# A retention layer fused with a two-layer MLP: two chunks' products with v per visit, the running state in fp32 on VectorE, a block-diagonal v for the short chunk

## The chip, the cores and the metric

The kernel runs on one NeuronCore of one Trainium2 chip. The core has a matrix engine (TensorE, PE; its weight loads are shown as PEld), VectorE (DVE), ScalarE (ACT), GpSimd (POOL) and SyncE (SP, which only issues transfers here). They run side by side, each in its own program order, and wait for one another by semaphores. The metric is device time in microseconds, smaller is better. All times below are in microseconds unless ns is written.

## What is computed

Per batch (8) and head (8), with 576 positions of 64 numbers, q, k and v give a causal product with decay. Its result, 4608 tokens of 512 numbers, goes through two matrix products with a nonlinear step between them:

```python
gamma = 1.0 - 2.0 ** (-5.0 - np.arange(H))
Dmat = np.where(rel >= 0, gamma[:, None, None] ** rel[None], 0.0)   # rel = i - j
attn = np.matmul(scale * np.matmul(q, k.T) * Dmat, v)
x = attn.transpose(0, 2, 1, 3).reshape(B * S, H * D)                 # 4608 x 512
h = x @ w_in                                                         # 512 x 2048
out = (h * np.cos(h)) @ w_out                                        # 2048 x 512
```

## The kernel before

**Chunks.** The positions of a batch are cut into chunks r = 0 to 4: four of 128 and a last one of 64, the short chunk. The decay is put into v (WV) and q (UP, UPN) ahead of time, so that a chunk needs four products, each for four pairs of heads c and the two heads hp of a pair:
- `scores` (line 515): k times q within the chunk, 64 contraction rows per head, into two PSUM banks (one per hp); `mask` (line 536), two VectorE multiplies with a triangular mask, writes them to RT as bf16
- `sums_q` (line 562): q times the state of all chunks before, a 128 by 128 block-diagonal state per pair (SB, bf16)
- `sums_v` (line 573): the masked scores times v, into the same PSUM bank as `sums_q`, and the copy of the sum to XT (the MLP's input)
- `state` (line 598): k times v, accumulated over the chunks in the PSUM bank ST; two ScalarE copies bring it to SB as bf16

`rest` (line 549) does sums_q, sums_v, state and the copies for one chunk. XT is copied by VectorE there (line 595), the state by ScalarE (line 616).

**The MLP.** Tokens go in nine blocks j of 512. `mlp1` (line 629) makes one of 16 column tiles of the hidden layer: four matmuls of 512 columns, the cosine on ScalarE (line 644), the product with h on VectorE (line 647). `mlp2` (line 654) makes a quarter of an output tile st (four of 16 matmuls of 512 columns); four quarters make one of four output tiles, which ScalarE copies out (osb, line 681), and `flush` stores from ScalarE's queue.

**PSUM.** Eight banks of 128 by 512 fp32: SC0 and SC1 (scores), PO (sums), ST (state), and four MM banks that `bank()` (line 212) hands out in turn, leaving out the one that an unfinished output tile holds. Nothing plans this: the order of the program is the order of each engine, and a bank is reused as soon as its last reader has signalled.

**The order around the change** is written out by hand in `emit` (line 714). In the loop over j from 1 on, the attention of batch b = j + 1 stands between the 16 quarters n of mlp2:
- j = 1 (batch 2): the short chunk of batch 1 and the scores of chunk 0 at n = 2, then one chunk and the next chunk's scores at n = 5, 8, 11, 14 (`stage`, line 622). For n under 8 two narrow mlp1 tiles of 192 columns (line 856) go ahead of each quarter
- j = 2 to 6 (batches 3 to 7): the short chunk of batch b - 1 and the scores of chunks 0 and 1 at n = 0; one chunk each at n = 4, 7, 10, 13; the scores of 2 and 3 behind n = 7's, of chunk 4 behind n = 13's. The second score pair of n = 0 and n = 7 takes two MM banks (line 850)
- j = 7: the short chunk of batch 7

**Inputs.** SP's queue loads k, q and v per chunk as fp32 (`load`, line 284). POOL casts k and multiplies q and v (`prep`, line 373), and SP's transposing transfers write KQT. `feed` does this one batch ahead, behind mlp1's tiles. Batches 0 and 1 have paths of their own through PE transposes.

Of the kernel before, what the change touches and what calls it, by code (L numbers as in the profile page):

```python
# [48 lines left out]
class Sched:  # L49


    def __init__(self, nc, es):
        self.nc, self.es = nc, es
        self.eng = {
            "dve": nc.vector, "act": nc.scalar, "pool": nc.gpsimd,
            "pe": nc.tensor, "sp": nc.sync,
        }
        self.sem = {k: es.enter_context(nc.semaphore(f"p_{k}")) for k in ("dve", "act", "pool", "pe")}
        self.count = dict.fromkeys(self.sem, 0)
        self.seen = {k: {} for k in self.eng}  # L60
# [38 lines left out]

    def op(self, eng, fn, reads=(), writes=()):  # L100
        self.waits(eng, reads, writes)
        return self.done(eng, fn(self.eng[eng]), reads, writes)
# [22 lines left out]
class _Kernel:  # L125
    def __init__(self, nc, es, q, k, v, w_in, w_out, out):
# [7 lines left out]
        def sb(name, shape, dt):  # L134
# [26 lines left out]
        self.VB = [[sb(f"vb{i}_{r}", [128, DM], BF16) for r in range(NCH)] for i in range(2)]  # L161
        self.bVB = [[Buf() for _ in range(NCH)] for _ in range(2)]
        self.RT = [[sb(f"rt{i}_{hp}", [128, 512], BF16) for hp in range(2)] for i in range(2)]
        self.bRT = [[Buf() for _ in range(2)] for _ in range(2)]
        self.SB = [sb(f"sb{i}", [128, NP * 128], BF16) for i in range(3)]
        self.bSB = [Buf() for _ in range(3)]
        self.GT = [sb(f"gt{i}", [128, 16 * TB], BF16) for i in range(2)]

# [10 lines left out]
        self.IG = sb("ig", [128, S_], F32)  # L179
        self.IP = sb("ip", [128, NCH], F32)  # L180
        self.UP = sb("up", [128, NP * S_], F32)
        self.WV = sb("wv", [128, NCH * H_], F32)
        self.UPN = sb("upn", [128, NCH * H_], F32)
        self.LW = sb("lw", [128, NCH * H_], F32)
        self.MK = sb("mk", [128, CH], BF16)
        self.ID = sb("ident", [128, 128], BF16)
        self.ZERO, self.bZERO = sb("zero", [128, 512], BF16), Buf()
# [41 lines left out]
    def consts_a(self):  # L229

        s = self.s
        bj = Buf()
        s.op("dve", lambda e: e.memset(self.JUNK.ap(), 0.0), writes=[bj])
        s.op("act", lambda e: e.activation(self.JUNK2.ap(), self.JUNK.ap(), AF.Exp), reads=[bj])
        s.op("pool", lambda e: e.iota(self.IP.ap(), [[CH, NCH]], base=0, channel_multiplier=1,
                                      allow_small_or_imprecise_dtypes=True), writes=[self.bIP])
# [12 lines left out]
        s.op("dve", lambda e: e.memset(self.C_PIH.ap(), float(math.pi / 2.0)), writes=[self.bC])  # L249
        for h in range(H_):  # L250
            s.op("dve", lambda e: e.tensor_scalar_mul(
                bass.AP(self.LW, h, [[NCH * H_, 128], [H_, NCH]]), self.IP.ap(), self.lng[h]),
                reads=[self.bIP], writes=[Buf()])
        self.bLW.w = [Tok("dve", "dve", s.count["dve"], {})]
        for i in range(3):
            s.op("dve", lambda e: e.memset(self.SB[i].ap(), 0.0), writes=[self.bSB[i]])

    def consts_n(self):
# [98 lines left out]
    def mul(self, eng, x, r, t, o, pitch, w, bw, bt):  # L357
# [3 lines left out]
            self.staged(x, r, [[D_, H_], [1, D_]]),  # L361
            bass.AP(w, r * H_, [[NCH * H_, ck], [1, H_], [0, D_]]), ALU.mult),
            reads=[self.bST32[x][r], bw], writes=[bt])
# [151 lines left out]
    def scores(self, b, r, later=False, sc=None):  # L515

        s, ck, i, q0 = self.s, ck_of(r), b % 2, CH * r
        sc = sc or list(zip(self.SC, self.bSC))
        mms = []
        for c in range(NP):  # L520
# [7 lines left out]
        self.group(mms, [self.bKT[i][r], self.bQT[i][r]], [sc[0][1], sc[1][1]])  # L528
        k = self.rt[b, r] = len(self.rt) % 2
        for hp in range(2):  # L530
# [12 lines left out]
    def masked(self, b, r, c, hp, ck):  # L543

        if b == 0 and r < NCH - 1:
            return bass.AP(self.GT[1], (2 * c + hp) * TB + r * CH, [[16 * TB, ck], [1, ck]])
        return bass.AP(self.RT[self.rt[b, r]][hp], c * CH, [[512, ck], [1, ck]])
# [8 lines left out]
    def sums(self, b, r, po=None, eng="dve"):  # L556

        if r:
            self.sums_q(b, r, po)
        return self.sums_v(b, r, po, eng)  # L560

    def sums_q(self, b, r, po=None):

# [5 lines left out]
                     bass.AP(self.KQT[i], TQ + c * S_ + q0, [[TP, 128], [1, ck]]),  # L569
                     dict(start=c == 0, stop=False, skip_group_check=True)) for c in range(NP)],  # L570
                   [self.bSB[(r - 1) % 3], self.bQT[i][r]], [bpo])

    def sums_v(self, b, r, po=None, eng="dve"):

        s, ck, i, q0 = self.s, ck_of(r), b % 2, CH * r
        po, bpo = po or (self.PO, self.bPO)
        mms = []
        for c in range(NP):
            for hp in range(2):
# [4 lines left out]
                    self.masked(b, r, c, hp, ck),  # L584
                    dict(start=r == 0 and c == 0, stop=c == NP - 1, skip_group_check=True)))
        reads = [self.bVB[i][r]]
        if b == 0 and r < NCH - 1:
# [4 lines left out]
        t0 = (b * S_ + q0) % XR  # L592
# [3 lines left out]
        return lambda: s.op(eng, fn, reads=[bpo], writes=self.bXT[t0 // GR:(t0 + ck) // GR])  # L596

# [23 lines left out]

    def stage(self, b, r):
        self.rest(b, r)
        if r + 1 < NCH:
            self.scores(b, r + 1)

# [87 lines left out]
    def emit(self):  # L714
# [138 lines left out]

# [38 lines left out]
```

## Time and profile before

| | |
|---|---|
| median of 3 runs | 312.69 (312.68 to 313.04) |
| the profiled execution | 312.78 |
| its span, first to last instruction | 311.0 |
| TensorE clock granted, mean | 0.995 of full |
| DMA engines, mean busy share | 9 tenths or more for slices 2 to 26 of 40 |
| VectorE: rt from sc, 128x512 | 36 of 682 ns |
| VectorE: xt from po, 128x512 | 26 of 691 ns |
| ScalarE: sb from st, 64x256 | 64 of 377 ns |
| ScalarE: osb from mm, 128x512 | 35 of 597 ns |

A page of the profile has the busy time of each engine, the span in 40 slices, the chain of work that ended last (followed back from the last instruction to what released each step), and the costliest groups of instructions by line. Besides it the trace answers with timelines (start, length, engine, line, operation, output from inputs, shapes, and in brackets the idle time before with what ended it). On VectorE neighbouring instructions overlap a little, so a start-to-start distance is shorter than a length.

### The profile page before, as it was taken

To read this page: it belongs to the slowest core of one execution; us is meant where nothing else is said; L and a number is where in the kernel's file an instruction comes from. 1 tells how busy PE (TensorE), PEld (TensorE's weight loads), DVE (VectorE), ACT (ScalarE), POOL (GpSimd) and SP (SyncE) were. 2 spreads that over 40 slices of the span, in tenths; PEclk is the share of its full clock that TensorE was granted. 3 is DMA by queue.
4 is the path that set the end of the run, shared out by engine and by line. 5 is a ranking of instruction groups with operands and counts; after the bars stand their busy time and mean duration, and the time that the engine had idled before them with its cause. 6 is when DMAs were issued, how large, how long until landed. Compare 5 with 4: busy or idle time off the path is not lost.

```text
span 311.0 us, 6450 instructions
## 1 busy us (share of the span) xinstructions
PE 303.1 (97%) x2538; PEld 159.0 (51%) x2538; DVE 178.3 (57%) x318; ACT 161.2 (52%) x288; POOL 106.5 (34%) x129
## 2 busy tenths in 40 slices
PE   6799999999999999999999999999999999999996
PEld 3574455666644455445544554455445554444444
DVE  5857644887548842785368554855487448405800
ACT  8658407875447433753277236723573347316711
POOL 4881046645565636354646554510000000000000
PEclk9979999999999999999999999999999999999999
DMA  7999999999999999999999998950101010120022
GB/s 230 252 198 208 208 216 247 250 229 182 249 222 179 233 208 228 181 229 200 251 195 221 237 222 195 191 136 34 36 0 70 34 36 0 40 98 0 1 76 95
DMA packets 138319, 49.12 MB, mean 158 GB/s; under 512 B 127921, under 2 KB 132273, under 8 KB 138289
## 3 DMA queue, kind: packets, MB, share of 16 engines
q1 hardware_dynamic: 128880, 34.88, 61.8%
q10 hardware_dynamic: 5184, 9.31, 8.9%
q0 software_dynamic: 4224, 4.52, 8.7%
q8 instruction: 20, 0.33, 0.5%
q14 instruction: 11, 0.08, 0.1%
HBM read 36.70 MB, written 9.44 MB: 148 GB/s over the span
## 4 chain that ended last, share of the span: by engine, by line
PE 92%; SPq 3%; DMA 2%; ACT 1%; DVE 0%; issue 0%; ACTq 0%
PE mm L511 62%; PE mm L513 20%; PE po L511 5%; PE sc L511 3%; DMA qn<-in_moe_w_in_dram 2%; SPq L288 2%; SPq L296 1%; PE st L511 1%; ACT osb L681 1%; PE po L513 0%; ACT kqt L415 0%; DVE win L330 0%; DVE xt L595 0%; ACT xt L595 0%; ACT sb L616 0%
## 5 line engine op out<-in xcount | busy, mean ns | idle before, releaser
L647 DVE TENSOR_TENSOR gt<-mm,cb 128x512 bf16<-128x512 f32 (+3 forms) x164 | 101.6, 626 | 61.2 <-ACT cb L644 58.6
L511 PE MATMUL mm<-xt,win 128*128 128x512 bf16 (+3 forms) x492 | 119.1, 353 | 0.5 <-DVE xt L595 0.4
L644 ACT ACTIVATE cb<-mm,c_pih 128x512 bf16<-128x512 f32 (+3 forms) x164 | 102.8, 636 | 31.1 <-PE mm L513 30.7
L511 PE MATMUL mm<-wout,gt 128*128 128x512 bf16 (+1 forms) x450 | 117.4, 373 | 0.0
L511 PEld LDWEIGHTS mm<-xt,win 128*128 128x128 bf16 x492 | 46.4, 98 | 48.8 <-DVE xt L595 1.0
L511 PEld LDWEIGHTS mm<-wout,gt 128*128 128x128 bf16 x450 | 41.0, 98 | 42.2 <-DVE gt L647 0.2
L513 PE MATMUL mm<-xt,win 128*128 128x512 bf16 (+3 forms) x164 | 57.9, 353 | 0.0
L513 PE MATMUL mm<-wout,gt 128*128 128x512 bf16 (+1 forms) x142 | 53.6, 378 | 0.0
L681 ACT ACTIVATE osb<-mm 128x512 f32<-128x512 f32 x35 | 20.9, 597 | 62.5 <-PE mm L513 62.5
L359 POOL TENSOR_TENSOR vb<-vn,wv 128x512 bf16<-128x512 f32 (+1 forms) x40 | 41.6, 1042 | 11.3 <-DMA vn<-in_v_dram 10.1
L595 DVE CAST xt<-po 128x512 bf16<-128x512 f32 (+1 forms) x34 | 21.3, 627 | 40.5 <-PE po L513 40.5
L370 POOL CAST kqb<-kn 128x512 bf16<-128x512 f32 (+1 forms) x35 | 21.3, 610 | 66.7 <-DMA kn<-in_k_dram 61.7
L616 ACT ACTIVATE sb<-st 64x256 bf16<-64x256 f32 x64 | 24.2, 377 | 35.7 <-PE st L513 34.7
L359 POOL TENSOR_TENSOR kqb<-qn,upn 128x512 bf16<-128x512 f32 (+1 forms) x30 | 31.3, 1042 | 14.5 <-DMA qn<-in_q_dram 13.6
L538 DVE TENSOR_TENSOR rt<-sc,mk 128x512 bf16<-128x512 f32 (+1 forms) x52 | 29.1, 597 | 6.5 <-PE sc L513 6.5
L513 PEld LDWEIGHTS mm<-xt,win 128*128 128x128 bf16 x164 | 16.0, 98 | 15.4
L513 PEld LDWEIGHTS mm<-wout,gt 128*128 128x128 bf16 x142 | 13.9, 98 | 16.5
L511 PE MATMUL po<-rt,vb 128*64 128x128 bf16 (+1 forms) x245 | 13.6, 220 | 0.0
L538 DVE TENSOR_TENSOR rt<-mm,mk 128x512 bf16<-128x512 f32 x20 | 12.8, 681 | 0.0
L511 PEld LDWEIGHTS po<-rt,vb 128*64 128x64 bf16 (+1 forms) x245 | 8.3, 108 | 5.5 <-DVE rt L538 2.1
L511 PE MATMUL sc<-kqt 64*128 64x128 bf16 (+1 forms) x196 | 10.3, 213 | 0.8 <-ACT kqt L415 0.8
L511 PE MATMUL st<-vb,kqb 128*64 128x64 bf16 x224 | 9.5, 198 | 1.5 <-POOL vb L359 0.8
(126 smaller groups left out, 166.5 us busy)
## 6 DMA issues: line engine op xcount, KB each, us to landing
out_dram<-osb ACTq DMA_DIRECT2D x35, 256.0 KB, 3.4
vn<-in_v_dram SPq DMA_DIRECT2D x32, 256.0 KB, 5.1
kn<-in_k_dram SPq DMA_DIRECT2D x28, 256.0 KB, 4.1
qn<-in_q_dram SPq DMA_DIRECT2D x24, 256.0 KB, 4.6
wout<-in_moe_w_out_dram POOLq DMA_DIRECT2D x4, 512.0 KB, 15.7
kn<-in_k_dram SPq DMA_DIRECT2D x4, 288.0 KB, 5.1
qn<-in_q_dram SPq DMA_DIRECT2D x4, 288.0 KB, 5.4
vn<-in_v_dram SPq DMA_DIRECT2D x8, 128.0 KB, 4.3
```

The source lines that it names most:

```text
L288: return self.s.dma(eng, f"{x}n{r}", lambda e: e.dma_start(dst, src), writes=[self.bST32[x][r]], after=after)
L296: self.s.dma("sp", f"{x}0_{c}", lambda e: e.dma_start(dst, src), writes=[self.bN0[x][c]])
L359: self.s.op(eng, lambda e: e.tensor_tensor(bass.AP(t, o, [[pitch, ck], [D_, H_], [1, D_]]), self.staged(x, r, [[D_, H_], [1, D_]]), bass.A ...
L370: fn = (lambda e: e.activation(o, f, AF.Copy)) if eng == "act" else (lambda e: e.tensor_copy(o, f))
L511: self.nc.tensor.matmul(o, a, b, **kw)
L513: return s.done("pe", self.nc.tensor.matmul(o, a, b, **kw), reads, writes)
L538: self.s.op("dve", lambda e: e.tensor_tensor(bass.AP(self.RT[k][hp], 0, p3), bass.AP(sc[0], 0, p3), bass.AP(self.MK, 0, [[CH, ck], [0, NP] ...
L595: fn = (lambda e: e.activation(o, f, AF.Copy)) if eng == "act" else (lambda e: e.tensor_copy(o, f))
L616: s.op("act", lambda e: e.activation(bass.AP(self.SB[r % 3], 64 * hp * 512 + 64 * hp, [[512, 64], [128, NP], [1, D_]]), bass.AP(self.ST, 6 ...
L644: s.op("act", lambda e: e.activation(co, mo, AF.Sin, bias=self.C_PIH.ap(), scale=1.0), reads=[bm, self.bC], writes=[bcb])
L647: s.op("dve", lambda e: e.tensor_tensor(bass.AP(g, dt * TB + o, [[16 * TB, 128], [1, n]]), mo, co, ALU.mult), reads=[bm, bcb], writes=bg[o ...
L681: s.op("act", lambda e: e.activation(o.ap(), m.ap(), AF.Copy), reads=[bm], writes=[bo])
```

## The change

1. **Two chunks per visit.** For batches 2 to 7, chunks 0 and 1 go together, and 2 and 3. `two` issues the q-times-state of the first, k times v of both (`kv`), the products with v of both, the scores that come next, and leaves the second chunk's q-times-state and its XT copy to `then`, which is called one or two quarters later. The second chunk's sums go to an MM bank.
2. **State in fp32.** k times v of each chunk is no longer accumulated in PSUM: each chunk has a half of ST, VectorE adds it to a running sum in SBUF (S32), and ScalarE copies that to SB (`add`).
3. **XT copies** of these chunks go to ScalarE.
4. **The short chunk.** Its scores of both heads of a pair are stacked in one bank (rows 0 to 63 and 64 to 127), masked by one VectorE instruction with a mask of its own (MK4), and multiplied with a block-diagonal v: four 128*128 matmuls (`sums_4`) in place of eight of 64*64. Its v is loaded by two transfers into the two halves of the rows, and multiplied by two POOL instructions of half the width; a POOL instruction that follows the second half, and the second half itself, wait for POOL's instruction before.
5. **Constants**: an extra column in IP, LW, WV, UPN for the second half, two zeroed v tiles, MK4.

The diff, cut to its core:

```diff
-    def op(self, eng, fn, reads=(), writes=()):
+    def op(self, eng, fn, reads=(), writes=(), shifted=False):
+        if eng == "pool":
+            if shifted or self.shifted:
+                self.need(eng, Tok(eng, eng, self.count[eng], {}))
+            self.shifted = shifted
...
+        for i in range(2):
+            s.op("dve", lambda e: e.memset(self.VB[i][NCH - 1].ap(), 0.0), writes=self.bV4[i])
+        for hp in range(2):
+            s.op("dve", lambda e: e.tensor_copy(
+                bass.AP(self.MK4, 64 * hp * 64, [[64, 64], [1, 64]]),
+                bass.AP(self.MK, 64 * hp * CH + 64 * hp, [[CH, 64], [1, 64]])),
...
     def scores(self, b, r, later=False, sc=None):
+        if r == NCH - 1:
+            m, bm = sc[0]
+            mms = []
+            for c in range(NP):
+                for hp in range(2):
+                    base = 64 * hp * TP + c * S_ + q0
+                    mms.append((
+                        bass.AP(m, 64 * hp * 512 + c * ck, [[512, ck], [1, ck]]),
...
+    def sums_4(self, b, r, po=None, eng="dve"):
+        ck, i, k = ck_of(r), b % 2, self.rt[b, r]
+        po, bpo = po or (self.PO, self.bPO)
+        self.group([(bass.AP(po, c * CH, [[512, 128], [1, ck]]),
+                     bass.AP(self.VB[i][r], c * 128, [[DM, 128], [1, 128]]),
+                     bass.AP(self.RT[k][0], c * ck, [[512, 128], [1, ck]]),
+                     dict(start=False, stop=c == NP - 1, skip_group_check=True))
+                    for c in range(NP)], self.bV4[i] + [self.bRT[k][0]], [bpo])
+        return self.evict_x(b, r, po, bpo, eng)
...
+    def kv(self, b, r):
+        i, o = b % 2, 256 * (r % 2)
...
+                    dict(start=not o and c == 0, stop=c == NP - 1, skip_group_check=True)))
+        self.group(mms, [self.bKB[i][r], self.bVB[i][r]], [self.bST])
+
+    def add(self, r):
+        s, k = self.s, r % 2
+        o = self.S32[k].ap()
+        f = self.ST[:, 256 * k:256 * k + 256]
+        if r == 0:
+            s.op("dve", lambda e: e.tensor_copy(o, f), reads=[self.bST], writes=[self.bS32[k]])
+        else:
+            s.op("dve", lambda e: e.tensor_tensor(o, f, self.S32[1 - k].ap(), ALU.add),
+                 reads=[self.bST, self.bS32[1 - k]], writes=[self.bS32[k]])
+        for hp in range(2):
+            s.op("act", lambda e: e.activation(
+                bass.AP(self.SB[r % 3], 64 * hp * 512 + 64 * hp, [[512, 64], [128, NP], [1, D_]]),
+                bass.AP(self.S32[k], 64 * hp * 256, [[256, 64], [D_, NP], [1, D_]]), AF.Copy),
+                reads=[self.bS32[k]], writes=[self.bSB[r % 3]] if hp else [Buf()])
+
+    def two(self, b, r, nxt):
+        if r:
+            self.sums_q(b, r)
+        self.kv(b, r)
+        self.kv(b, r + 1)
+        po = self.bank()
+        done = self.sums_v(b, r, eng="act")
+        self.sums_v(b, r + 1, po, first=True)
+        self.add(r)
+        done()
+        for k, sc in nxt:
+            self.scores(b, k, sc=sc and sc())
+        self.add(r + 1)
+
+        def then():
+            self.sums_q(b, r + 1, po, first=False)
+            self.evict_x(b, r + 1, *po, "act")()
+        return then
+
+    def both(self):
+        return [self.bank(), self.bank()]
...
+            at = (8, 13) if j == 1 else (5, 11)
...
-                if j == 1:
-                    if n == 2:
-                        self.rest(1, NCH - 1)
-                        self.scores(2, 0)
-                    elif n % 3 == 2:
-                        self.stage(2, n // 3 - 1)
-                elif n == 0 and b <= B_:
+                if n == (1 if j == 1 else 0) and b <= B_:
                     self.rest(b - 1, NCH - 1)
-                if 1 < j < B_ - 1:
-                    if n in (4, 7, 10, 13):
-                        self.rest(b, n // 3 - 1)
-                    if n in (0, 7):
-                        self.scores(b, n // 3)
-                        self.scores(b, n // 3 + 1, sc=[self.bank(), self.bank()])
-                    elif n == 13:
-                        self.scores(b, NCH - 1)
+                if j < B_ - 1:
+                    if j == 1 and n == 3:
+                        self.scores(b, 0)
+                        self.scores(b, 1, sc=[(self.PO, self.bPO), (self.ST, self.bST)])
+                    elif j > 1 and n == 0:
+                        self.scores(b, 0)
+                        self.scores(b, 1, sc=self.both())
+                    if n == at[0]:
+                        then = self.two(b, 0, [(2, None), (3, self.both)])
+                    elif n == at[1]:
+                        then = self.two(b, 2, [(4, None)])
+                    elif n in (at[0] + 1, at[1] + 2):
+                        then()
```

More of the change, by code (lines that the diff above doesn't have):

```diff
@@ L17 @@
 NCH = (S_ + CH - 1) // CH
+NW = NCH + 1
 TOK = B_ * S_
@@ L61, in __init__ @@
         self.dsem = {}
+        self.shifted = False
     def need(self, eng, tok):
@@ L162, in __init__ @@
         self.bVB = [[Buf() for _ in range(NCH)] for _ in range(2)]
+        self.bV4 = [[Buf(), Buf()] for _ in range(2)]
+        self.bS4 = [Buf(), Buf()]
         self.RT = [[sb(f"rt{i}_{hp}", [128, 512], BF16) for hp in range(2)] for i in range(2)]
@@ L166, in __init__ @@
         self.bSB = [Buf() for _ in range(3)]
+        self.S32 = [sb(f"s32_{i}", [128, NP * D_], F32) for i in range(2)]
+        self.bS32 = [Buf(), Buf()]
         self.GT = [sb(f"gt{i}", [128, 16 * TB], BF16) for i in range(2)]
@@ L179, in __init__ @@
         self.IG = sb("ig", [128, S_], F32)
-        self.IP = sb("ip", [128, NCH], F32)
+        self.IP = sb("ip", [128, NW], F32)
         self.UP = sb("up", [128, NP * S_], F32)
-        self.WV = sb("wv", [128, NCH * H_], F32)
-        self.UPN = sb("upn", [128, NCH * H_], F32)
-        self.LW = sb("lw", [128, NCH * H_], F32)
+        self.WV = sb("wv", [128, NW * H_], F32)
+        self.UPN = sb("upn", [128, NW * H_], F32)
+        self.LW = sb("lw", [128, NW * H_], F32)
         self.MK = sb("mk", [128, CH], BF16)
+        self.MK4, self.bMK4 = sb("mk4", [128, 64], BF16), Buf()
         self.ID = sb("ident", [128, 128], BF16)
@@ L194, in __init__ @@
         self.bUP = [Buf() for _ in range(NP)]
+        self.bIP4 = [Buf(), Buf()]
         def ps(name):
@@ L234, in consts_a @@
         s.op("act", lambda e: e.activation(self.JUNK2.ap(), self.JUNK.ap(), AF.Exp), reads=[bj])
-        s.op("pool", lambda e: e.iota(self.IP.ap(), [[CH, NCH]], base=0, channel_multiplier=1,
+        s.op("pool", lambda e: e.iota(self.IP[:, 0:NCH], [[CH, NCH]], base=0, channel_multiplier=1,
                                       allow_small_or_imprecise_dtypes=True), writes=[self.bIP])
@@ L249, in consts_a @@
         s.op("dve", lambda e: e.memset(self.C_PIH.ap(), float(math.pi / 2.0)), writes=[self.bC])
+        for hp in range(2):
+            s.op("dve", lambda e: e.tensor_scalar_add(
+                self.IP[64 * hp:64 * hp + 64, NCH:NW], self.IP[64 * hp:64 * hp + 64, NCH - 1:NCH],
+                -64.0 * hp), reads=[self.bIP], writes=[self.bIP4[hp]])
         for h in range(H_):
             s.op("dve", lambda e: e.tensor_scalar_mul(
-                bass.AP(self.LW, h, [[NCH * H_, 128], [H_, NCH]]), self.IP.ap(), self.lng[h]),
-                reads=[self.bIP], writes=[Buf()])
+                bass.AP(self.LW, h, [[NW * H_, 128], [H_, NW]]), self.IP.ap(), self.lng[h]),
+                reads=[self.bIP] + self.bIP4, writes=[Buf()])
         self.bLW.w = [Tok("dve", "dve", s.count["dve"], {})]
@@ L256, in consts_a @@
             s.op("dve", lambda e: e.memset(self.SB[i].ap(), 0.0), writes=[self.bSB[i]])
+        for i in range(2):
[4 more added lines that the diff above has]
+                bass.AP(self.MK, 64 * hp * CH + 64 * hp, [[CH, 64], [1, 64]])),
+                reads=[self.bMK], writes=[self.bMK4] if hp else [Buf()])
     def consts_n(self):
@@ L285, in load @@
         ck = ck_of(r)
+        if x == "v" and r == NCH - 1:
+            for hp in range(2):
+                dst = bass.AP(self.XN[x], 64 * hp * NCH * DM + r * DM,
+                              [[NCH * DM, ck], [D_, NP], [1, D_]])
+                src = bass.AP(self.src[x], ((b * H_ + hp) * S_ + CH * r) * D_,
+                              [[D_, ck], [2 * S_ * D_, NP], [1, D_]])
+                self.s.dma(eng, f"vs{hp}", lambda e: e.dma_start(dst, src),
+                           writes=[self.bS4[hp]], after=after)
+            return
         dst = self.staged(x, r, [[D_, H_], [1, D_]])
@@ L349, in vmul @@
         i = b % 2
+        if r == NCH - 1:
+            for hp in range(2):
+                p = 64 * hp
+                self.s.op(eng, lambda e: e.tensor_tensor(
+                    bass.AP(self.VB[i][r], p * DM + p, [[DM, 64], [2 * D_, NP], [1, D_]]),
+                    bass.AP(self.XN["v"], p * NCH * DM + r * DM, [[NCH * DM, 64], [D_, NP], [1, D_]]),
+                    bass.AP(self.WV, p * NW * H_ + NCH * H_ + hp, [[NW * H_, 64], [2, NP], [0, D_]]),
+                    ALU.mult), reads=[self.bS4[hp], self.bWV], writes=[self.bV4[i][hp]], shifted=hp == 1)
+            return
         self.mul(eng, "v", r, self.VB[i][r], 0, DM, self.WV, self.bWV, self.bVB[i][r])
@@ L361, in mul @@
             self.staged(x, r, [[D_, H_], [1, D_]]),
-            bass.AP(w, r * H_, [[NCH * H_, ck], [1, H_], [0, D_]]), ALU.mult),
+            bass.AP(w, r * H_, [[NW * H_, ck], [1, H_], [0, D_]]), ALU.mult),
             reads=[self.bST32[x][r], bw], writes=[bt])
@@ L518, in scores @@
         sc = sc or list(zip(self.SC, self.bSC))
+        k = self.rt[b, r] = len(self.rt) % 2
+        if r == NCH - 1:
+            m, bm = sc[0]
+            mms = []
+            for c in range(NP):
+                for hp in range(2):
+                    base = 64 * hp * TP + c * S_ + q0
+                    mms.append((
+                        bass.AP(m, 64 * hp * 512 + c * ck, [[512, ck], [1, ck]]),
+                        bass.AP(self.KQT[i], base, [[TP, 64], [1, ck]]),
+                        bass.AP(self.KQT[i], TQ + base, [[TP, 64], [1, ck]]),
+                        dict(start=c == 0, stop=c == NP - 1, skip_group_check=True)))
+            self.group(mms, [self.bKT[i][r], self.bQT[i][r]], [bm])
+            p3 = [[512, 128], [ck, NP], [1, ck]]
+            s.op("dve", lambda e: e.tensor_tensor(
+                bass.AP(self.RT[k][0], 0, p3), bass.AP(m, 0, p3),
+                bass.AP(self.MK4, 0, [[ck, 128], [0, NP], [1, ck]]), ALU.mult),
+                reads=[bm, self.bMK4], writes=[self.bRT[k][0]])
+            return
         mms = []
@@ L528, in scores @@
         self.group(mms, [self.bKT[i][r], self.bQT[i][r]], [sc[0][1], sc[1][1]])
-        k = self.rt[b, r] = len(self.rt) % 2
         for hp in range(2):
@@ L543, in masked @@
     def masked(self, b, r, c, hp, ck):
-        if b == 0 and r < NCH - 1:
+        if b == 0:
             return bass.AP(self.GT[1], (2 * c + hp) * TB + r * CH, [[16 * TB, ck], [1, ck]])
@@ L559, in sums, with sums_q @@
             self.sums_q(b, r, po)
-        return self.sums_v(b, r, po, eng)
-    def sums_q(self, b, r, po=None):
+        return (self.sums_v if r < NCH - 1 else self.sums_4)(b, r, po, eng)
+    def sums_q(self, b, r, po=None, first=True):
         ck, i, q0 = ck_of(r), b % 2, CH * r
@@ L569, in sums_q, with sums_v @@
                      bass.AP(self.KQT[i], TQ + c * S_ + q0, [[TP, 128], [1, ck]]),
-                     dict(start=c == 0, stop=False, skip_group_check=True)) for c in range(NP)],
+                     dict(start=first and c == 0, stop=not first and c == NP - 1,
+                          skip_group_check=True)) for c in range(NP)],
                    [self.bSB[(r - 1) % 3], self.bQT[i][r]], [bpo])
-    def sums_v(self, b, r, po=None, eng="dve"):
-        s, ck, i, q0 = self.s, ck_of(r), b % 2, CH * r
+    def sums_v(self, b, r, po=None, eng="dve", first=None):
+        ck, i = ck_of(r), b % 2
         po, bpo = po or (self.PO, self.bPO)
+        first = r == 0 if first is None else first
         mms = []
@@ L584, in sums_v @@
                     self.masked(b, r, c, hp, ck),
-                    dict(start=r == 0 and c == 0, stop=c == NP - 1, skip_group_check=True)))
+                    dict(start=first and c == 0, stop=c == NP - 1, skip_group_check=True)))
         reads = [self.bVB[i][r]]
-        if b == 0 and r < NCH - 1:
+        if b == 0:
             reads += [x for bs in self.bR0 for x in bs]
@@ L591, in sums_v, with evict_x @@
         self.group(mms, reads, [bpo])
-        t0 = (b * S_ + q0) % XR
+        return self.evict_x(b, r, po, bpo, eng)
[7 more added lines that the diff above has]
+                    for c in range(NP)], self.bV4[i] + [self.bRT[k][0]], [bpo])
+        return self.evict_x(b, r, po, bpo, eng)
+    def evict_x(self, b, r, po, bpo, eng):
+        ck = ck_of(r)
+        t0 = (b * S_ + CH * r) % XR
         o = bass.AP(self.XT, t0, [[NP * XR, 128], [XR, NP], [1, ck]])
@@ L595, in sums_v @@
         fn = (lambda e: e.activation(o, f, AF.Copy)) if eng == "act" else (lambda e: e.tensor_copy(o, f))
-        return lambda: s.op(eng, fn, reads=[bpo], writes=self.bXT[t0 // GR:(t0 + ck) // GR])
+        return lambda: self.s.op(eng, fn, reads=[bpo], writes=self.bXT[t0 // GR:(t0 + ck) // GR])
     def state(self, b, r):
@@ L620, in state @@
         return evict
[L622 to L625, printed above, removed]
+    def kv(self, b, r):
+        i, o = b % 2, 256 * (r % 2)
+        mms = []
+        for c in range(NP):
+            for hp in range(2):
+                h = 2 * c + hp
+                mms.append((
+                    bass.AP(self.ST, 64 * hp * 512 + o + c * D_, [[512, 64], [1, D_]]),
+                    bass.AP(self.KQB[i], 2 * DM * r + h * D_, [[NCH * 2 * DM, CH], [1, D_]]),
+                    bass.AP(self.VB[i][r], h * D_, [[DM, CH], [1, D_]]),
+                    dict(start=not o and c == 0, stop=c == NP - 1, skip_group_check=True)))
[9 more added lines that the diff above has]
+                 reads=[self.bST, self.bS32[1 - k]], writes=[self.bS32[k]])
+        for hp in range(2):
+            s.op("act", lambda e: e.activation(
[21 more added lines that the diff above has]
+        return [self.bank(), self.bank()]
     def mlp1(self, j, dt, o=0, n=TB):
```

## The prediction

> **What bounds the kernel now.** I read the page first. PE is busy for 97% of the span and carries 92% of the chain that ended last. DVE and ACT are busy for little more than half of it, POOL for a third.
>
> ```profile
> PE 303.1 (97%) x2538; PEld 159.0 (51%) x2538; DVE 178.3 (57%) x318; ACT 161.2 (52%) x288; POOL 106.5 (34%) x129
> ...
> PE 92%; SPq 3%; DMA 2%; ACT 1%; DVE 0%; issue 0%; ACTq 0%
> ```
>
> After the first 20 us PE's longest wait is 0.76, so whatever lengthens or shortens PE's own queue moves the end one for one. Second view, PE's timeline. Between 512-column matmuls (0.216 us from start to start) stand the attention visits. First two small groups amid out-projection matmuls, then the ends of a whole visit (line 847, j = 3, n = 7):
>
> ```profile
> 46.66 0.38 PE L513 MATMUL mm<-wout,gt 128*128 128x512 bf16 x1
> 46.88 0.33 PE L511 MATMUL po<-ident,kqb 128*128 128x128 bf16 x3
> 47.05 0.22 PE L513 MATMUL po<-ident,kqb 128*128 128x128 bf16 x1
> 47.10 0.81 PE L511 MATMUL mm<-wout,gt 128*128 128x512 bf16 x3
> 47.75 0.38 PE L513 MATMUL mm<-wout,gt 128*128 128x512 bf16 x1
> 48.06 0.39 PE L511 MATMUL sc<-kqt 64*128 64x128 bf16 x7
> 48.24 0.22 PE L513 MATMUL sc<-kqt 64*128 64x128 bf16 x1
> 48.39 0.39 PE L511 MATMUL mm<-wout,gt 128*128 128x512 bf16 x1
> ...
> 176.62 0.38 PE L513 MATMUL mm<-wout,gt 128*128 128x512 bf16 x1
> 176.84 0.33 PE L511 MATMUL po<-kqt,sb 128*128 128x128 bf16 x3
> ...
> 178.18 0.61 PE L511 MATMUL mm<-wout,gt 128*128 128x512 bf16 x2
> ```
>
> The columns are start, length, engine, line, operation, tiles, the part of the array in use (128*128, 64*128 and so on) and the shapes. A group of four 128*128 matmuls costs 47.10 - 46.66 - 0.216 = 0.22: its own columns. The score group (four pairs, 0.056 a pair, 0.22) costs 48.39 - 47.75 - 0.216 = 0.42: 0.20 more, for two changes of shape. So **a change of shape costs 0.10 to 0.12**; I take 0.105.
>
> Third view, VectorE's and then ScalarE's timeline behind the same visit at j = 2:
>
> ```profile
> 145.81 1.28 DVE L538 TENSOR_TENSOR rt<-sc,mk 128x512 bf16<-128x512 f32 x2
> 147.00 1.28 DVE L538 TENSOR_TENSOR rt<-mm,mk 128x512 bf16<-128x512 f32 x2
> ...
> 145.32 0.78 ACT L616 ACTIVATE sb<-st 64x256 bf16<-64x256 f32 x2 [2.60 <-PE st L513]
> ```
>
> Four masks start 0.598 apart, 2.39 for the four; two state copies take 0.78. Nobody waits for them now.
>
> **PE's own work.** Pieces from those starts: q times state (q) 0.22, for the short chunk 0.12; products with v (v) 0.22; k times v (kv) 0.12; scores (sc) 0.22, short 0.12. They rebuild the visit at n = 7: 0.22 + 0.22 + 0.12 + 2 x 0.22 + 3 changes x 0.105 = 1.32, against 178.18 - 176.62 - 0.216 = 1.34 in the trace.
>
> Before, a batch of j = 2 to 6 has five visits of 1.01, 0.56, 1.34, 0.79 and 1.03: 4.73, with 13 changes of shape. After, in the order of the changed code:
> - n = 0: short q 0.12, short v 0.12 (now 128*128: no change before it), two sc 0.45, 2 changes: 0.90
> - n = 5: two kv, two v, two sc, 3 changes: 1.46
> - n = 6: q, no change: 0.22
> - n = 11: q, two kv, two v, short sc, 3 changes: 1.35
> - n = 13: q: 0.22
>
> That is 4.15, 8 changes: 0.58 less, 2.9 over five batches. For j = 1: five visits of 0.78, 0.89, 1.12, 1.12, 1.03 = 4.94 before, 4.15 after: 0.79. The short chunks of batches 0 and 7 lose two changes each, 0.45 to 0.24: 0.4. **Gain: 4.1 us.**
>
> **The wait that it makes.** In two() for chunks 0 and 1, chunk 1's product with v goes to a bank taken from the four that the MLP uses, and the next score pair takes the two after it. Following bank() through j = 2: mm1 holds chunk 1, mm2 and mm3 the scores of chunk 3, mm0 the open output tile. The next output tile, at n = 8, gets mm1. It must be empty by then. Who empties it: ScalarE's xt copy in then(), and ScalarE works in program order, behind the state copies of chunk 1 (add(1)), behind VectorE's add, which stands behind all four masks of the chunks 2 and 3. With T0 the first kv:
> - kv, kv end their starts at 0.23; VectorE starts 0.26 after a group's last start (148.88 to 149.14 for xt in the trace): add(0) from 0.49 to 0.91
> - first v 0.26 to 0.49, second to 0.71, a change, scores from 0.81: the first mask starts at 1.26
> - four masks of 0.598: add(1) starts at 3.65; by the 128x256 rows (mean 0.425) it ends at 4.08
> - two state copies from 4.15 (0.40 a start), xt copy from 4.96 (0.60, osb and xt rows): the bank is free at 5.56, PE sees it at 5.62 (0.06, as after the kqt copy at 53.94)
> - PE gets there at 1.37 + 0.87 (n = 5) + 0.22 (q) + 2 x 0.86 = 4.19
>
> **PE waits 1.43 at n = 8**, in each of five batches: 7.15. In j = 1 the pair stands at n = 8 and the bank comes back at n = 12, one group later (5.06): 0.56. There, too, n = 3 now issues two score groups instead of one, and four masks go ahead of the MLP products of the 192-column tiles on VectorE. From that visit's start: masks 0.55 to 2.94, the product of dt = 6 ends at 3.29; PE wants its bank for dt = 9 at 0.66 + 0.33 + 0.33 + 0.86 + 0.33 = 2.52: 0.83. Behind these PE has no slack that would take any of it back.
>
> **What lies beside other work, at nothing.** 24 xt copies move from VectorE (0.69 each) to ScalarE (0.60) and 24 adds come to VectorE. Apart from the wait above this is hidden: while PE does the out-projection, ScalarE idles 62.5 us in all before its osb copies. q times state at n = 6 needs state 0, copied by 1.8 after T0, and comes at 2.24; without that 0.4 of cover PE would wait for as long as it is late. The short chunk's v: one more DMA issue on SP's queue per batch (0.65 to 1.2 there) for the same bytes, ahead of the next transposes, and two POOL multiplies of half the width with a wait for POOL itself, behind which the next casts stand; the short multiply of batch 3 ends at 99.7 and its product comes at 137, so 37 us cover it. Score pairs that come earlier (chunk 3 of batch 2, from 85 to about 81) need a transpose that SP had issued by 73.6. The new constants on VectorE (two memsets of 0.27, four small ones of up to 0.17) stand in its 1.60 idle before 5.40.
>
> **Sum.** 312.78 (the profiled execution; span 311.0, 1.8 around it; median of the runs 312.69) - 4.1 + 7.15 + 0.56 + 0.83 = 317.2.
>
> **Bounds.** The add has no row of its own: 0.34 (gt 128x192, 0.353) to 0.49 (gt 128x320). The state copy reads SBUF now: 0.36 (the fastest sb) up to 0.48, by the up row (SBUF to SBUF, 0.86 for 576 elements, scaled); I take 0.38, the row nearest in size. Both together move the wait at n = 8 by -0.15 to +0.3, five times. Two kv side by side may cost 0.12 to 0.2 each; a change 0.10 to 0.12. The sum's own range is 315.5 to 319.5.
>
> **Rivals.**
> *No wait (faster).* If chunk 1's bank is free by 4.19 after T0, only the 0.83 of j = 1 is left against the gain: 309.5. For it: VectorE's rows are upper ends, since neighbours overlap. Against: the chain would have to be 1.43 shorter, over two masks, and the masks' spacing is read from the same four instructions. It decides from a chain of 4.2. Chance 0.10; and 0.03 that a wait of half the length leaves it within 0.2% (about what a measurement of this kernel can tell from no change).
>
> *The clock falls behind each wait.* Idle times of 0.69 and 0.81 between 12.7 and 15.6 ended with half the clock. Busy times by window (length, then PE, PEld, DVE, ACT, POOL, and the granted clock):
>
> ```profile
> 12.00:15.40 3.40, 1.94 (x29) 0.87 (x23) 3.40 (x6) 1.62 (x4) 3.38 (x4) 1.00 0.94 202
> 15.40:18.90 3.50, 3.28 (x48) 2.55 (x48) 1.23 (x3) 2.12 (x5) 3.50 (x5) 0.51 1.16 193
> ...
> 52.90:56.30 3.40, 2.64 (x38) 1.83 (x33) 2.36 (x4) 2.25 (x6) 2.40 (x3) 1.00 1.17 339
> ```
>
> A window with PE busy 1.94 of 3.40 us was followed by a clock of 0.51; one with 2.64 of 3.40 kept 1.00. A wait of 1.43 leaves about 1.97 of 3.40 busy, at the losing end, but with full-width matmuls. If it falls each time, 3.4 us at half speed lose 1.7, six times: 327. The Trainium skill ("TensorE: Matmul & The Clock Gate", Why this matters for your kernels) warns only of idle gaps over about 3 us; by it the clock stays and 317.2 holds. The drop at 15.4 came with less than that. Chance 0.06.
>
> *The changes of shape save less.* If side by side kv, or the stacked scores, cost what was saved, the gain is 1 to 2 and the time 319 to 320.5. Against: the rebuilt visits fit to 0.02. Chance 0.07.
>
> **How the numbers follow.** Forecast 0.74. Range 314.8 to 320.5: the sum's range, with a margin below and the last rival above; no wait, half a wait and the clock case (0.19) stay out. Faster 0.10, within 0.2% 0.03, slower 0.87.
>
> **What would show it.** Right: out-projection matmuls that wait 1.2 to 1.7 us for ScalarE's xt copy, once in each of j = 2 to 6, and 0.5 at j = 1; one PE wait for VectorE's product in j = 1; visits of 1.46 and 1.35; a granted clock of 1.00 after 20 us. Wrong: the first matmul at n = 8 that starts 0.216 after its neighbour, a clock of 0.5 behind the waits, or PE waits for POOL or for transposes.

## The result, and the profile after

The changed kernel takes 317.43 us (median of four runs, 316.80 to 319.28) against 312.87 for the kernel before: a ratio of 1.0138, 95% interval 1.0089 to 1.0187. The profiled execution is the slowest of its runs, 319.28 with a span of 317.5; about 2.0 of its 6.5 over the span before come ahead of 41 us, where the executions of all these kernels differ among themselves (the last section). The rest, 4.5, is what the medians show.

The page after, the same two lines as before (busy times; the chain that ended last, by engine):

```profile
PE 296.2 (93%) x2470; PEld 156.3 (49%) x2506; DVE 170.6 (54%) x316; ACT 176.6 (56%) x312; POOL 108.4 (34%) x137
...
PE 81%; DVE 6%; ACT 4%; SPq 3%; DMA 2%; issue 2%; ACTq 0%
```

PE's share fell from 97% to 93%, and 10% of the chain now lies on VectorE and ScalarE: PE waits. (Some matmul records are missing from this trace, so PE's count and busy time are a little low.) Where it waits, PE's timeline of j = 3 shows. The columns are start, length, engine, line, operation, tiles, array part, shapes, and in brackets the idle time with what ended it:

```profile
145.03 0.38 PE L558 MATMUL mm<-wout,gt 128*128 128x512 bf16 x1
145.34 0.31 PE L556 MATMUL st<-vb,kqb 128*64 128x64 bf16 x7
...
149.32 0.38 PE L558 MATMUL mm<-wout,gt 128*128 128x512 bf16 x1
150.97 0.82 PE L556 MATMUL mm<-wout,gt 128*128 128x512 bf16 x3 [1.27 <-ACT xt L676]
```

The visit's first kv starts at 145.34, T0 of the prediction. The output tile of n = 8 could start at 149.32 + 0.216 = 149.54 and starts at 150.97: 1.43 late (the bracket's 1.27 counts from the modelled end of the matmul before), released by ScalarE's xt copy. VectorE's, then ScalarE's timeline beside it:

```profile
145.82 0.42 DVE L723 COPY s<-st 128x256 f32<-128x256 f32 x1 [1.39 <-PE st L558]
146.60 1.29 DVE L602 TENSOR_TENSOR rt<-sc,mk 128x512 bf16<-128x512 f32 x2 [0.35 <-PE sc L558]
147.80 1.28 DVE L602 TENSOR_TENSOR rt<-mm,mk 128x512 bf16<-128x512 f32 x2
149.00 0.41 DVE L725 TENSOR_TENSOR s<-st,s 128x256 f32<-128x256 f32 x1
...
149.44 0.42 ACT L729 ACTIVATE sb<-s 64x256 bf16<-64x256 f32 x1 [1.69 <-DVE s L725]
...
150.32 0.60 ACT L676 ACTIVATE xt<-mm 128x512 bf16<-128x512 f32 x1
```

Read from top to bottom this is the chain: four masks, the add behind them, two state copies (149.44 and 149.88) of which the first waited 1.69 for the add, and the xt copy, which needed none of these and only stands behind them. The distance from the short chunk of one batch to that of the next is the cleanest measure, since it leaves out the start: 32.41 before, 33.29 after, the same five times over.

### The profile page after: what moved, and what is told of

It is laid out like the page before. It is cut to its first block, busy times and chain, and to the rows that moved or that the text cites. A ratio compares the mean times of both kernels' runs of the same rounds, so it can differ in the third digit from the quotient of the medians.

```text
span 317.5 us, 6394 instructions
## 1 busy us (share of the span) xinstructions
PE 296.2 (93%) x2470; PEld 156.3 (49%) x2506; DVE 170.6 (54%) x316; ACT 176.6 (56%) x312; POOL 108.4 (34%) x137
## 4 chain that ended last, share of the span: by engine, by line
PE 81%; DVE 6%; ACT 4%; SPq 3%; DMA 2%; issue 2%; ACTq 0%
PE mm L556 56%; PE mm L558 19%; DVE rt L602 5%; PE sc L556 3%; DMA qn<-in_moe_w_in_dram 2%; PE po L556 2%; SPq L324 2%; PE st L556 2%; ACT xt L676 1%; ACT sb L729 1%; SPq L332 1%; DVE s L725 1%; ACT osb L812 1%; ACT kqt L460 0%; PE po L558 0%
## 5 line engine op out<-in xcount | busy, mean ns | idle before, releaser
L556 PE MATMUL mm<-wout,gt 128*128 128x512 bf16 (+1 forms) x424 | 111.5, 372 | 10.2 <-ACT xt L676 6.8
L558 PE MATMUL mm<-wout,gt 128*128 128x512 bf16 (+1 forms) x142 | 53.6, 377 | 0.2
L729 ACT ACTIVATE sb<-s 64x256 bf16<-64x256 f32 x48 | 19.9, 415 | 35.5 <-DVE s L725 29.0
L404 POOL TENSOR_TENSOR vb<-vn,wv 128x512 bf16<-128x512 f32 x32 | 33.3, 1043 | 15.5 <-DMA vn<-in_v_dram 14.1
L602 DVE TENSOR_TENSOR rt<-sc,mk 128x512 bf16<-128x512 f32 x32 | 20.6, 683 | 7.7 <-PE sc L558 7.7
L558 PEld LDWEIGHTS mm<-xt,win 128*128 128x128 bf16 x164 | 16.2, 99 | 15.4
L725 DVE TENSOR_TENSOR s<-st,s 128x256 f32<-128x256 f32 x18 | 7.5, 417 | 28.1 <-PE st L558 28.1
L602 DVE TENSOR_TENSOR rt<-mm,mk 128x512 bf16<-128x512 f32 x22 | 14.0, 679 | 0.0
L389 POOL TENSOR_TENSOR vb<-vn,wv 64x256 bf16<-64x256 f32 x16 | 9.8, 614 | 4.0 <-PE po L558 3.3
L556 PE MATMUL sc<-kqt 64*128 64x128 bf16 (+1 forms) x182 | 9.6, 213 | 1.0 <-ACT kqt L460 0.8
L556 PE MATMUL st<-vb,kqb 128*64 128x64 bf16 x224 | 7.7, 200 | 1.5 <-POOL vb L404 0.8
L556 PEld LDWEIGHTS st<-vb,kqb 128*64 128x64 bf16 x224 | 5.8, 113 | 5.4 <-issue 3.8
```

The source lines that it names most:

```text
L389: self.s.op(eng, lambda e: e.tensor_tensor(bass.AP(self.VB[i][r], p * DM + p, [[DM, 64], [2 * D_, NP], [1, D_]]), bass.AP(self.XN["v"], p ...
L404: self.s.op(eng, lambda e: e.tensor_tensor(bass.AP(t, o, [[pitch, ck], [D_, H_], [1, D_]]), self.staged(x, r, [[D_, H_], [1, D_]]), bass.A ...
L556: self.nc.tensor.matmul(o, a, b, **kw)
L558: return s.done("pe", self.nc.tensor.matmul(o, a, b, **kw), reads, writes)
L602: self.s.op("dve", lambda e: e.tensor_tensor(bass.AP(self.RT[k][hp], 0, p3), bass.AP(sc[0], 0, p3), bass.AP(self.MK, 0, [[CH, ck], [0, NP] ...
L725: s.op("dve", lambda e: e.tensor_tensor(o, f, self.S32[1 - k].ap(), ALU.add), reads=[self.bST, self.bS32[1 - k]], writes=[self.bS32[k]])
```

## The experiments

All times are medians beside runs of the kernel before on the same chip (312.87 to 313.07); "distance" is the one just named, in the steady batches.

| | time | ratio (95%) | distance |
|---|---|---|---|
| changed kernel | 317.43 | 1.0138 (1.0089 to 1.0187) | 33.29 |
| e1, add ahead of the masks | 311.03 | 0.9921 (0.9893 to 0.9950) | 31.84 |
| e2, xt copy ahead of the state copies | 309.67 | 0.9904 (0.9871 to 0.9936) | 31.84 |
| e3, xt copy on VectorE | 312.45 | 0.9990 (0.9968 to 1.0012) | 32.38 |
| e4, short chunk alone | 312.42 | 0.9981 (0.9960 to 1.0002) | 32.28 |
| e5, e2 with two changes of shape more | 311.64 | 0.9944 (0.9918 to 0.9970) | 32.06 |
| e6, e2 with split first scores | 310.23 | 0.9908 (0.9876 to 0.9941) | 31.84 |
| e7, masks of chunk 3 twice | 330.27 | 1.0552 (1.0514 to 1.0591) | 34.74 or 36.43 |
| e8, masks of chunk 3 three times | 346.08 | 1.1057 (1.1007 to 1.1108) | 37.70 to 37.96 |
| e9, visits at n = 8 and 13 | 313.40 | 1.0010 (0.9991 to 1.0029) | 32.43 |
| e10, e6 with batch 3's visits at 8 and 13 | 309.34 | 0.9883 (0.9857 to 0.9910) | 31.84 |

**e1: the add ahead of the masks.**

```diff
+        self.add(r + 1)
         for k, sc in nxt:
             self.scores(b, k, sc=sc and sc())
-        self.add(r + 1)
```

> The changed kernel with one thing moved: VectorE's add for the second chunk (and ScalarE's two state copies behind it) stands ahead of the masks of the next scores instead of behind them. Theory (PE waits at n = 8 for the bank of chunk 1, whose copy stands on ScalarE behind state copies that wait for an add behind four masks): the bank is free at about 3.9 us after the visit's first kv, PE comes at 4.19, so the wait of 1.44 in five batches and the 0.58 at j = 1, n = 12 are gone: 317.4 - 7.2 - 0.6 = 309.6, under the kernel before. Rival (it is the masks of the scores themselves that hold the next output tile's bank): the masks end 0.3 later than before, so 317.4 to 319. Rival (ScalarE has too much to do with the xt copies): nothing moves, 317.4.

VectorE's, ScalarE's and PE's timeline in the same batch (first kv at 141.07):

```profile
142.02 0.42 DVE L725 TENSOR_TENSOR s<-st,s 128x256 f32<-128x256 f32 x1
142.36 1.28 DVE L602 TENSOR_TENSOR rt<-sc,mk 128x512 bf16<-128x512 f32 x2
...
144.40 0.60 ACT L676 ACTIVATE xt<-mm 128x512 bf16<-128x512 f32 x1
...
145.06 0.38 PE L558 MATMUL mm<-wout,gt 128*128 128x512 bf16 x1
145.28 0.59 PE L556 MATMUL mm<-wout,gt 128*128 128x512 bf16 x2
```

The distance fell by 1.45, the wait, to 0.57 under the kernel before. The xt copy ends at 145.00, and PE starts the tile of n = 8 at 145.28, 0.22 behind its neighbour: it no longer waits for the copy at all. The masks start 1.29 after the first kv, against 1.26 in the changed kernel (0.3 later had been expected), so they hold their own banks for as long as before; ScalarE's load is the same. Both rivals fall. The median, 311.03, is above the 309.6 expected although the profiled run (309.23) is not, and this profile doesn't show why: its distances from j = 2 on are all 31.84. Two things that vary from execution to execution are seen in e6 and in the last section.

**e2: the xt copy ahead of the state copies.** VectorE keeps the changed kernel's order; add() without its copies, which move into then():

```diff
         def then():
             self.sums_q(b, r + 1, po, first=False)
             self.evict_x(b, r + 1, *po, "act")()
+            self.copies(r + 1)
```

> The changed kernel with the second chunk's two state copies on ScalarE moved behind the xt copy of that chunk; VectorE's order (masks, then add) is as in the changed kernel. Theory: ScalarE's xt copy no longer stands behind the masks and the add, bank free at about 3.4 after the first kv, PE never waits for it: 309.6, as in the other order. If the masks' own time on VectorE held PE, nothing changes: 317.4. If ScalarE's load did it, nothing changes either.

ScalarE's timeline, and then PE's at n = 8:

```profile
143.56 0.60 ACT L676 ACTIVATE xt<-mm 128x512 bf16<-128x512 f32 x1 [0.26 <-PE mm L558]
145.00 0.85 ACT L735 ACTIVATE sb<-s 64x256 bf16<-64x256 f32 x2 [0.84 <-DVE s L725]
...
144.87 0.38 PE L558 MATMUL mm<-wout,gt 128*128 128x512 bf16 x1
145.08 0.81 PE L556 MATMUL mm<-wout,gt 128*128 128x512 bf16 x3
```

The xt copy now runs as soon as its matmuls are done and is over 0.9 before PE asks (145.08, which is 0.216 behind 144.87: no wait). The state copies wait for the add as before, 0.84, and nobody waits for them. So the 7.8 us came from the xt copy's place behind state copies that wait for a late add: moving the copy alone (here) or the add (e1) takes the wait away.

**e3: the xt copy on VectorE.**

```diff
-            self.evict_x(b, r + 1, *po, "act")()
+            self.evict_x(b, r + 1, *po, "dve")()
```

> The changed kernel with the xt copy of the second chunk on VectorE instead of ScalarE. Theory: the copy still stands behind four masks and the add (starts about 4.0 after the first kv), but no longer behind two state copies: bank free at about 4.7 against PE's 4.19, a wait of 0.5 in five batches and none at j = 1: 317.4 - 7.2 - 0.6 + 2.7 = 312.3. If only ScalarE's load counted, the wait would be gone: 309.6. If the masks' banks held PE, 317.4.

VectorE's xt copy, and PE behind it:

```profile
146.86 0.68 DVE L676 CAST xt<-mm 128x512 bf16<-128x512 f32 x1
...
146.85 0.38 PE L558 MATMUL mm<-wout,gt 128*128 128x512 bf16 x1
147.60 0.82 PE L556 MATMUL mm<-wout,gt 128*128 128x512 bf16 x3 [0.37 <-DVE xt L676]
```

147.60 - 146.85 - 0.216 = 0.53 of wait, 0.5 expected; 312.45 measured, 312.3 expected. An intermediate chain gives an intermediate wait, and at j = 1 none, as expected (36.43 there, as in e1).

**e9: the visits two or three quarters later.** Only the line that places them changes:

```diff
-            at = (8, 13) if j == 1 else (5, 11)
+            at = (8, 13)
```

> The changed kernel with its pair visits moved: at n = 8 and 13 in every j (in the changed kernel only at j = 1), not at 5 and 11. Nothing else: VectorE's and ScalarE's orders stay. Theory: the chain that empties chunk 1's bank is as long as before (5.6 after the visit's first kv), but the next output tile asks for it at n = 12, one group of 0.86 later than n = 8 asked (5.06 against 4.19): the wait falls from 1.44 to 0.58, the distance from batch to batch from 33.29 to 32.42, the time from 317.4 to 313.1. Rival (the wait is not of this bank, or not of this chain): 33.29 and 317.4, or no wait at all and 31.84.

PE's timeline in the same batch:

```profile
150.59 0.38 PE L558 MATMUL mm<-wout,gt 128*128 128x512 bf16 x1
151.39 0.39 PE L556 MATMUL mm<-wout,gt 128*128 128x512 bf16 x1 [0.42 <-ACT xt L676]
```

32.43 and 313.40: the same chain, asked for one group later, costs 151.39 - 150.59 - 0.216 = 0.58 instead of 1.43.

**e4: the short chunk's part alone.** The loop over j, the visits and the state are those of before; scores, sums_4, the loads and the multiplies of the short chunk are those of the change.

> The kernel before with the short chunk's part of the change alone (stacked scores, one mask, block-diagonal v, its two loads and two multiplies, the constants); the visits, the state and the xt copies are those of before. Theory (a change of shape on PE costs 0.105): one change less per batch in j = 1 to 6 and two less for batches 0 and 7, 6 x 0.115 + 2 x 0.22 = 1.1 us less: 311.7, and the profile shows a visit of 0.45 falling to 0.23. Rival (the new constants and the second short load at the start push the first MLP tile back): 312.9 or more, with the loss before 25 us.

Batch 0's short chunk on PE:

```profile
38.79 0.38 PE L558 MATMUL mm<-wout,gt 128*128 128x512 bf16 x1
...
39.12 0.25 PE L556 MATMUL po<-rt,vb 128*128 128x64 bf16 x3
...
39.24 0.81 PE L556 MATMUL mm<-wout,gt 128*128 128x512 bf16 x3
```

39.24 - 38.79 - 0.216 = 0.23; before it was 0.45. All matmuls are 128*128, and no change of shape is left. The distance falls by 0.13 (0.115 expected) and the profiled run by 0.8 (312.78 to 311.97); the median falls by 0.5, with an interval that touches no change. The spans (first to last instruction) of its runs have a median of 310.2 against 311.2, 1.0 less, near the 1.1 expected; about 2.2 of the time lie outside the span in these runs, 1.8 in those of the kernel before, and what these 0.4 are stays open. The rival is not seen: the first MLP tile starts at 18.4.

**e5: two changes of shape more.** The same matmuls in another order:

```diff
+        self.kv(b, r)
         if r:
             self.sums_q(b, r)
-        self.kv(b, r)
         self.kv(b, r + 1)
```

> The variant with the xt copy ahead of the second state copies, with one thing more: in the visit of chunks 2 and 3 the q-times-state group stands between the two k-times-v groups instead of ahead of them. The same matmuls, two changes of shape on PE more per batch. Theory (each costs 0.105): the distance from batch to batch goes from 31.84 to 32.05, six batches: 309.7 + 1.3 = 311.0. Rival (a change costs nothing by itself and the visits got shorter because groups of one kind stand side by side): 31.84 and 309.7, or any other distance.

The distance is 32.06: 0.22 for two changes, 0.11 each. This is the price of a change by itself. The time, 311.64, is 0.6 over the one expected, and in this profile one distance is longer: 33.52 into j = 3. PE's matmuls there, and the transfer that SP issued:

```profile
112.09 0.38 PE L556 MATMUL mm<-kqt 64*128 64x128 bf16 x7 [1.28 <-ACT xt L676]
...
107.61 2.18 SPq L426 DMA_TRANSPOSE kqt<-kqb  x1
```

These are the scores of batch 3's chunk 3. The bracket names the xt copy, which had long been done; the group also waits for its transposed k and q, whose transfer was issued at 107.61 and landed at 111.95, 1.3 after PE asked.

**e6: the first scores of j = 1 apart.**

```diff
                     if j == 1 and n == 3:
                         self.scores(b, 0)
+                    elif j == 1 and n == 5:
                         self.scores(b, 1, sc=[(self.PO, self.bPO), (self.ST, self.bST)])
```

> The variant with the xt copy ahead of the second state copies, and at j = 1 the scores of chunk 1 go to n = 5 instead of n = 3 beside those of chunk 0. Theory (four masks in a row stand ahead of the MLP products on VectorE and hold a bank for 0.69): the wait at j = 1 is gone, two changes of shape more: 309.7 - 0.7 + 0.2 = 309.2, all of it between the short chunks of batches 1 and 2 (36.44 to about 35.95). Rival (that wait comes from the banks' order, not from the masks): 36.44 or 36.65 there, 309.9.

In the changed kernel the wait of j = 1 is this one, with 0.08 from start to start of 192-column matmuls: 76.34 - 75.43 - 0.08 = 0.83.

```profile
75.43 0.25 PE L558 MATMUL mm<-xt,win 128*128 128x192 bf16 x1
76.34 0.34 PE L556 MATMUL mm<-xt,win 128*128 128x192 bf16 x2 [0.66 <-DVE gt L778]
```

In e6 it is gone, and 36.44 became 35.81 (35.95 expected). With two changes of shape more (0.22) that is 0.85 less: the wait was made by four masks in a row. But the median did not fall, 310.23 against 309.67, and in the profile the distance from batch 2 to batch 3 is 32.60: the same transfer landed at 110.7, asked for at 110.1. Over the profiles it lands at 108.8 to 112.1; the kernel before asked for it at 113.0 and had 3.75 to spare, the pair visit at n = 5 asks at 110.1 to 110.6 in e1, e2, e5 and e6, and in two of these four the transfer was late. In the changed kernel (landed at 112.1, asked at 113.1) the waits of j = 1 hid it.

**e10: batch 3's visits later.** With e6's code:

```diff
-            at = (8, 13) if j == 1 else (5, 11)
+            at = (8, 13) if j <= 2 else (5, 11)
```

> The variant with the xt copy ahead of the second state copies and the split first scores, and batch 3's visits at n = 8 and 13 like batch 2's. In two profiles of the last runs the scores of batch 3's chunk 3 waited 0.6 and 1.3 for its transposing transfer, which lands at 108.8 to 112.1 while the pair visit asks for it at 110.1. Theory: 2.6 later the transfer has landed in every execution; the distance from batch 2 to batch 3 is 31.84 in the profile too, the time 309.1 with a smaller spread than 308.8 to 314.9. Rival (those runs spread for reasons at the start): the same spread, 309.5 to 310.5.

The distance from batch 2 to 3 is 31.84, the transfer lands 3.7 ahead of the request, the spread is 308.19 to 310.52. At 309.34 this beats both kernels: the change's own gain without its wait. Its median doesn't stand clear of e2's 309.67, and six runs are few to call the spread smaller.

**e7 and e8: a longer wait.** The masks of chunk 3 are issued twice, or three times, writing the same values:

```diff
-                self.mask(k, hp, ck, sc[hp])
+                for _ in range(2 if b > 1 and r == 3 else 1):
+                    self.mask(k, hp, ck, sc[hp])
```

> The changed kernel with the two masks of chunk 3 (batches 2 to 7) issued twice, the second time writing the same values again: the wait at n = 8 grows by two masks, from 1.44 to 2.6 to 2.9. Theory (the wait is that chain, one for one): distance from batch to batch 33.29 + 1.2 to 1.5 = 34.5 to 34.8, about 325. The rival by which PE's clock falls to half behind a wait (not seen at 1.44): 1.7 per batch more, 36.3, about 335. By the Trainium skill (TensorE: Matmul & The Clock Gate), idle gaps under about 3 us keep the clock.

> The same with the two masks of chunk 3 issued three times: a wait of 3.9 to 4.3. With the clock kept: distance 35.7 to 36.2, about 333. With the clock at half for 3.4 behind each wait: 1.7 more per batch, 37.4 to 37.9, about 343. The Trainium skill's rule for the clock gate (gaps over about 3 us) would make it fall here.

In e7 PE idles 2.73 by the trace's bracket (1.27 in the changed kernel). The distance is 34.74 three times, as expected with the clock kept, and 36.43 twice: 1.69 more. Busy times of e7 by window (length, PE, PEld, DVE, ACT, POOL, granted clock), for a wait of each kind and the 3.4 us behind it:

```profile
116.50:120.10 3.60, 0.98 (x5) 0.51 (x6) 1.02 (x2) 1.91 (x4) 2.65 (x3) 1.00 1.12 243
120.10:123.50 3.40, 3.40 (x11) 1.26 (x9) 0.00 (x0) 0.00 (x0) 1.36 (x2) 0.50 1.00 218
152.00:155.40 3.40, 0.81 (x4) 0.20 (x2) 1.94 (x4) 1.34 (x4) 1.73 (x2) 1.00 0.98 161
155.50:158.90 3.40, 3.36 (x38) 1.85 (x40) 0.00 (x0) 0.47 (x1) 1.65 (x2) 1.00 1.19 251
```

The same idle time costs the clock in one batch (0.50 for 3.4 us) and not in another. In e8, idle for 4.18 (4.33 from start to start), the clock fell in all five steady batches: 37.70 to 37.96, 1.5 to 1.8 over the 36.2 of a kept clock (31.84 and the wait). The times, 330.27 and 346.08, lie between the two expectations for e7 and 3 over the higher one for e8, whose clock was at half for 6.8 in j = 1.

What decides shows when the falls are laid side by side. In e8's steady batches the clock falls at 126.92, 164.47, 202.02, 239.56 and 277.11: 37.55 apart, though most of the batches are 37.87 or more apart. In e7 it falls at 120.09 and 225.90, 105.81 apart. A stretch at half lasts 3.41; 37.55 is 11 times that and 105.81 is 31 times. So the falls stand on a raster of 3.41 that doesn't follow the kernel's work. Windows cut on this raster (the same columns), four of e7, then two of e8's j = 1:

```profile
116.68:120.09 3.41, 0.97 (x5) 0.51 (x6) 0.87 (x2) 1.91 (x4) 2.65 (x3) 1.00 1.16 251
120.09:123.50 3.41, 3.41 (x11) 1.26 (x9) 0.00 (x0) 0.00 (x0) 1.36 (x2) 0.50 1.00 218
188.36:191.77 3.41, 1.49 (x7) 0.70 (x8) 0.36 (x2) 1.91 (x4) 0.45 (x1) 1.00 1.09 228
191.77:195.19 3.42, 3.42 (x55) 2.09 (x54) 1.18 (x3) 1.00 (x3) 1.60 (x3) 1.00 1.14 276
...
85.96:89.37 3.41, 1.28 (x6) 0.39 (x4) 2.96 (x5) 0.34 (x1) 2.02 (x4) 1.00 0.81 175
89.37:92.78 3.41, 2.22 (x8) 0.95 (x8) 0.00 (x0) 1.57 (x4) 2.44 (x3) 0.50 1.19 278
```

In e7's three batches that kept the clock the gap lies across two windows and leaves PE busy for 1.49 or more in each. In the two that lost it, and in e8's falls, one window had at most 1.28, that is, 2.13 or more of idle. So the same gap is cheap or dear by where it falls.

## Why the prediction was right

The forecast, 317.2 in a range of 314.8 to 320.5, met 317.43 (4.4 forecast over the kernel before, 4.6 measured), and by its own mechanism:

- **The wait at n = 8**: 1.43 forecast, 1.43 in the trace of j = 3, with a bracket of 1.27 or 1.28 in each of the five batches. (By the short chunks' times, the prediction's rows at 145.81 and 176.62, called j = 2 and j = 3, are of j = 3 and j = 4; nothing in the sum hangs on it.) Its steps from T0: first mask 1.26 forecast and 1.26 measured, add(1) 3.65 and 3.66, state copies 4.15 and 4.10, xt copy 4.96 and 4.98, PE released 5.62 and 5.63. e1, e2, e3 and e9 change one link each (the add's place, the copies' place, the xt copy's engine, the time of the request), and the wait follows: 0, 0, 0.53, 0.58.
- **The gain on PE**: 0.58 per batch forecast, 0.57 in e1 and e2, where the wait is gone. The visits at n = 5 and 11, forecast at 1.46 and 1.35, take 1.47 in e8 and 1.38 in e7, which have the same visits and no record missing there. A change of shape at 0.105 is borne out by e4 (the short chunk) and measured alone in e5 (0.11).
- **The rest**: 0.56 at j = 1, n = 12 forecast, 0.58 measured; 0.83 for the four masks at j = 1, 0.83 in the trace from start to start, and e6 takes it away. State copies from SBUF cost 415 ns, not 377, inside the bounds.
- **Costed at nothing, rightly**: POOL's self-waits, the second short load, the constants. The first MLP matmul of twelve profiles lies at 18.2 to 20.3, the kernel before at 19.3 within them.
- **Costed at nothing, wrongly**: the score pairs that come earlier. I took batch 2's transfer, with seven us to spare, and not batch 3's, which had 3.75 and loses most of it. The changed kernel does not show it, because its waits come first; e5 and e6 do.
- **The rival of the clock** was no rival at this length: the clock stayed at 1.00 behind every wait of 1.43. e7 and e8 show that its price, 1.7, was about right (1.5 to 1.8). Its reading of the start doesn't carry over: there a window with PE busy for 1.94 of 3.40, with small matmuls, was followed by half the clock, and in e7 one with 1.49 of 3.41, between 512-column matmuls, was not. That first fall, at 15.4, also came inside the second of the two gaps that the prediction names (14.8 to 15.6), not behind it.
- **One sign did not come as written**: a granted clock of 1.00 after 20 us. In the profiled run it was at half from 19.8 to 23.2, at the start, where no wait of the change lies.

## What to carry to other kernels

Before two pieces of work share a visit, write down for every buffer that goes back to a common pool which instruction frees it, on which engine, and everything that stands ahead of it there: the freeing copy belongs ahead of work that nobody waits for. Groups of small matmuls that use the array in the same shape are worth putting side by side, at 0.1 us a change. And a step that is pulled forward by 2.6 us wants its inputs checked in the batch where the loads are latest, not in the next one at hand.

## What the runs showed of the hardware

- A change of the array part in use costs PE 0.10 to 0.12 us, and a group of 128*128 matmuls between 128*128 matmuls costs only its columns (0.22 for four of 128, 0.12 for four of 64).
- PE's clock between 512-column matmuls: idle for 1.27 in each of five batches it kept 1.00; idle for 2.73 it fell in two of five; for 4.18 in all five, each time to 0.50 for 3.4 us, with 1.5 to 1.8 us lost. The falls of e7 and of e8 stand on a raster of 3.41 us; the clock was kept behind windows of it with up to 1.92 us of idle and fell behind all with 2.13 or more. The Trainium skill ("TensorE: Matmul & The Clock Gate", Why this matters for your kernels) warns of idle gaps over about 3 us. The trace agrees for 4.18, but 2.73 already cost the clock in two of five batches, so gaps under 3 us don't always keep it, as e7's expectation had it from that page. The same page of the Trainium skill (What's actually happening) says that the activity window, 3413 ns, runs freely; the raster of 3.41 agrees.
- The start varies from execution to execution: in twelve profiles the first input-weight tile reaches VectorE between 16.4 and 18.9 (17.8 before, 18.9 in the changed kernel), and the clock is at half for 3.4 us there in some of them (15.4 to 18.9 before, 19.8 to 23.2 in the changed kernel, where denser work stands). These two may make the 1.9 us by which its profiled run is over its median; that was not tried.
